# Reordering the first transfers of a Strassen-style GEGLU feed-forward kernel

## The chip, the cores and the metric

The kernel runs on one core of a Trainium2 chip. The metric is the device time of one execution in microseconds (us). The time before is 273.48 us, the median of three runs from 273.24 to 274.23 us. The profiled execution took 273.29 us, and its trace spans 271.5 us from the first to the last instruction. All positions in time below are microseconds from the start of that span.

A core has five engines with instruction streams of their own: TensorE (PE; its weight loads are listed apart as PEld), VectorE (DVE), ScalarE (ACT), GpSimd (POOL) and SyncE (SP). SP and ACT also issue transfers; their issue work is listed as SPq and ACTq. Sixteen DMA engines move the data.

## The reference

All inputs are bf16. The tokens are flattened to 1024 rows.

```python
B, S, D, F = 32, 32, 1024, 3584        # x: (B, S, D); w_gate, w_up: (D, F); w_down: (F, D)

def _gelu(x):
    return jax.nn.gelu(x, approximate=True)

def reference(x, w_gate, w_up, w_down):
    return (_gelu(x @ w_gate) * (x @ w_up)) @ w_down
```

## The kernel before, in words

**What is computed where.** The kernel does both stages (gate and up together, then down) by a Strassen-like scheme of block sums, with products of 128x128 weights against 128x512 moving columns. Stage one treats the gate matrix and the up matrix as two block columns and splits the inner dimension of 1024 into two halves of `KD` = 4 blocks of 128. The transposed activations lie in four tiles, `b11`, `b12` (first half of the inner dimension, token halves 0 and 1) and `b21`, `b22` (second half). Each has 4 blocks of 128 rows and 512 columns.

**The start.** One of the products, the lower half of the gate matrix (`a12`) by `b21`, needs no block sums. The kernel does it ahead for the first 24 blocks of 128 gate columns: six groups of four (`a12_ahead`, indices 0 to 5). Groups 0 and 1 are in tiles named `a12a`, the rest in `a12b`. Each group's tile holds 4 blocks of 128 rows, `k` = 0 to 3, with 512 columns; one such block is 128 KB and is called a gate row block here.

`b21` is filled in two ways. Its blocks 0 and 1 (`KQ` = 2) come as plain copies of x into `x_nat` (`load_nat`, L198, one transfer of 128 KB for each block), are transposed on PE against an identity matrix (`transposed`, L262), and are copied out of PSUM by DVE (L269). Its blocks 2 and 3 come by one transposing transfer (`load_xT(0, KD + KQ, DT)`, L226, issued at L219). The other three tiles of x come by transposing transfers later on.

**What sets the order.** The order is written out by hand: inside `tc.manual_schedule()` each engine runs its instructions in program order, and semaphores between engines and transfers are derived from the tiles that are read and written. Transfers issued by one engine go through that engine's queue in order. Before the change the queues begin so:

- SP: block 0 of `x_nat` (L205); group 0, `k` = 0 (L223); group 0, `k` = 1 (L225); the transposing transfer for blocks 2 and 3 of `b21` (L226); group 0, `k` = 2 and 3; group 1, `k` = 2 and 3 (L230); groups 2 and 3 in halves; the first chunk's up and gate weights (L238); group 4; two more transposing transfers; group 5; the last transposing transfer; the second chunk's weights.
- ACT: a probe of 0.5 KB (L208); block 1 of `x_nat` (L224); group 1, `k` = 0 and 1 (L227); then a table load and a one-column `gelu` (L254) that brings the table in before it is needed.
- POOL: constants and the identity matrix; then nothing until the first block sums, which wait for up weights.

PE begins with `NWARM` = 6 matmuls on constants (L258). It transposes block 0 (four transposes, L266), runs `NFILL` = 4 short matmuls on constants (L273), and goes into the loop at L331:

```python
for k in range(KQ):
    for half in range(2):
        for j in range(KB):
            product_ahead(ps[0][j], 0, j, k, k + 1, slice(half * HALF * P, (half + 1) * HALF * P))
        if k == half == 0:
            transposed(1)
for j in range(KB):
    product_ahead(ps[1][j], 1, j, 0, KQ)
for i in (0, 1):
    for j in range(KB):
        product_ahead(ps[i][j], i, j, KQ)
```

So the needs come in this order: group 0 `k` = 0 with block 0 of `b21`; block 1 of `x_nat`; group 0 `k` = 1; group 1 `k` = 0 and 1; then blocks 2 and 3 of `b21` with group 0 `k` = 2 and 3; then group 1 `k` = 2 and 3; then groups 2 to 5 and the chunks (L368). All matmuls of the products have line L288 or L277 in the profile, since helpers record them.

Of the kernel before, what the change touches and what calls it, by code (L numbers as in the profile page):

```python
# [8 lines left out]
ACT = mybir.ActivationFunctionType  # L9
# [4 lines left out]
def kernel(  # L14
# [20 lines left out]
    nc = tc.nc  # L35
    P = nc.NUM_PARTITIONS
    fp32 = mybir.dt.float32
    f32r = mybir.dt.float32r
    bf16 = mybir.dt.bfloat16
# [7 lines left out]
    NB = 512  # L47
    assert N == 2 * NB and D == 2 * NB and F % (4 * P) == 0
    DT, FT = D // P, F // P
    KD = DT // 2  # L50
# [4 lines left out]
    KQ = DT // 4  # L55
    HF = FT // 2
    MT = NB // P
    NWARM = 6
    NFILL = 4
    KB = 4  # L60
    QF = HF // 2
    batches = [(0, KB), (KB, QF), (QF, QF + KB), (QF + KB, HF)]
# [12 lines left out]
    ework = one.enter_context(tc.tile_pool(name="ework", bufs=2))  # L75
# [37 lines left out]
    a12_ahead = [ring.tile([P, KD, KB * P], bf16, name="a12a", tag="ring") for _ in range(2)]  # L113
    b11 = xpool.tile([P, KD, NB], bf16, name="b11")
    b21 = xpool.tile([P, KD, NB], bf16, name="b21")
# [74 lines left out]
    ident = xpool.tile([P, P], bf16, name="ident")  # L190
    make_identity(nc, ident)
    NB_P = NB // P
# [4 lines left out]
    with tc.manual_schedule():  # L197
        def load_nat(eng, dt, p0, p1):  # L198
            eng.dma_start(  # L199
                out=x_nat[:, p0:p1, dt * P : (dt + 1) * P],  # L200
                in_=xf[p0 * P : p1 * P, (KD + dt) * P : (KD + dt + 1) * P].rearrange("(b p) d -> p b d", p=P),
            )
# [7 lines left out]
        def load_ahead(i, k0, k1, eng=nc.sync, j0=0, j1=KB):  # L210
            f0 = i * KB
            eng.dma_start(
                out=a12_ahead[i][:, k0:k1, j0 * P : j1 * P],
                in_=wg_r[:, KD + k0 : KD + k1, (f0 + j0) * P : (f0 + j1) * P],
            )

        def load_xT(nb, d0, d1):
            t = ((b11, b12), (b21, b22))[d0 // KD][nb]
            nc.sync.dma_start_transpose(  # L219
                out=t[:, d0 % KD : (d1 - 1) % KD + 1, :], in_=xf[nb * NB : (nb + 1) * NB, d0 * P : d1 * P]  # L220
            )

        load_ahead(0, 0, 1)  # L223
        load_nat(nc.scalar, 1, 0, NB_P)  # L224
        load_ahead(0, 1, 2)  # L225
        load_xT(0, KD + KQ, DT)  # L226
        load_ahead(1, 0, KQ, nc.scalar)  # L227
        a12_ahead += [spool.tile([P, KD, KB * P], bf16, name="a12b", tag=t) for t in ("s2", "s4", "s1", "s3")]
        for i in (0, 1):
            load_ahead(i, KQ, KD)  # L230
        def load_halves(i):
            for k in range(0, KD, KQ):
                load_ahead(i, k, k + KQ)
# [3 lines left out]
        for which in (1, 0):  # L237
            load_w_all(0, which)  # L238
        load_ahead(4, 0, KD)
        load_xT(0, 0, KD)  # L240
        load_xT(1, 0, KD)
        for j0 in range(0, KB, KB // 2):
            load_ahead(5, 0, KD, j0=j0, j1=j0 + KB // 2)
# [1 line left out]
        for which in (1, 0):  # L245
            load_w_all(1, which)

        def gelu(src, tag, bufs):
            h = ework.tile([P, NB], bf16, name=tag, tag=tag, bufs=bufs)[:, : src.shape[-1]]
            nc.scalar.activation(h, src, ACT.Gelu_apprx_tanh)  # L250
            return h


        gelu(ident[:, :1], "h0", 6)  # L254

        warm_ps = acc("A")
        for _ in range(NWARM):
# [4 lines left out]
        def transposed(dt):  # L262
            for half, tp in enumerate(tps[dt]):
                p0 = half * HALF
                for b in range(HALF):
                    nc.tensor.transpose(  # L266
                        tp[:, b * P : (b + 1) * P], x_nat[:, p0 + b, dt * P : (dt + 1) * P], ident
                    )
                nc.vector.tensor_copy(b21[:, dt, p0 * P : (p0 + HALF) * P], tp)  # L269

        transposed(0)
        for _ in range(NFILL):
            nc.tensor.matmul(warm_ps[:, :P], lhsT=ones_w, rhs=ones_w, start=True, stop=True)  # L273
# [41 lines left out]
        def first_product(ft):  # L315
            psa = acc("A")
            prod(psa, quads(*chunk_of(ft))[0], b11, True)
            if ft < NAHEAD:
                return psa, gelu(added(ahead_at[ft], psa), "h0", 6)
            return psa, snap(psa, "sn1", 4)  # L320
# [34 lines left out]
        tt(t2, b22, t1, SUB)  # L355
        group_ahead(5, "CCAA", between=lambda: nc.scalar.copy(b22r, b22))
        begun = {ft: (psa, gelu(c, "h0", 6)) for ft, (psa, c) in begun.items()}
        tt(t3, b22, b12, SUB)
        next(chunk0)
# [8 lines left out]
        for ci in range(NCH):  # L368
# [8 lines left out]
            sn5, sn2, h1, h0 = [], [], [], []  # L377
# [17 lines left out]
            if fts[-1] < NAHEAD:  # L395
                h0 = first
# [228 lines left out]
```

## Time and profile before

| What | Value |
|---|---|
| Time, median of three runs | 273.48 us |
| Time of the profiled execution | 273.29 us |
| Its span | 271.5 us |
| PE busy | 267.4 us (98%) |
| DVE busy | 202.8 us (75%) |
| ACT busy | 115.6 us (43%) |
| POOL busy | 120.2 us (44%) |
| Granted TensorE clock, mean | 1.000 |
| Bytes moved by DMA | 35.86 MB, 132 GB/s on average |

Busy shares are of the span. A matmul's recorded duration includes the fill and drain of the array and overlaps the next one, so the pace of a run of matmuls is read from start to start. A transfer has two times: how long the issuing engine is occupied (the SPq and ACTq entries) and how long after the begin of the issue its data has landed (the median in the table of issues). Where a group of issues is only one transfer, the median is that transfer's own time.

### The profile page before, as it was taken

Reading aid. Unit: us, or ns where it says so; the run is one execution under the profiler, and the core shown is the slowest. Engines: PE = TensorE matmul, PEld = TensorE weight load, DVE = VectorE, ACT = ScalarE, POOL = GpSimd, SP = SyncE. Lnnn points to the kernel's source line nnn. Section 1 sums busy time; section 2 is a strip of 40 time slices with the busy share of each in tenths; the row PEclk is TensorE's granted clock in tenths of the full one; section 3 lists DMA queues with packets and bytes.
Section 4 is the critical chain, followed back from the end, with each engine's and each line's share of the span. In section 5 each row is a group of like instructions: output and inputs, shape, how many; then the busy total and the mean of one; then the engine's idle time right before and its main releaser. Section 6 shows DMA issues by size and latency. Waiting matters only on the chain.

```text
span 271.5 us, 3422 instructions
## 1 busy us (share of the span) xinstructions
PE 267.4 (98%) x1216; PEld 192.9 (71%) x1216; DVE 202.8 (75%) x205; ACT 115.6 (43%) x189; POOL 120.2 (44%) x60
## 2 busy tenths in 40 slices
PE   8999999999999999999999999999999999999995
PEld 4444776886787788688688687764458888888883
DVE  1448998886876876876776478469999999998621
ACT  2435766445544643745636635434000307870000
POOL 1090099977995994994994996000000000000000
DMA  7999230514505505505224290006981537865211
GB/s 173 325 245 251 52 104 21 150 38 117 157 1 153 156 2 155 139 15 157 81 76 127 49 325 4 0 2 202 356 253 60 158 112 260 273 196 163 73 42 58
DMA packets 56672, 35.86 MB, mean 132 GB/s; under 512 B 9936, under 2 KB 56656, under 8 KB 56656
## 3 DMA queue, kind: packets, MB, share of 16 engines
q1 hardware_dynamic: 53264, 33.17, 43.2%
q10 hardware_dynamic: 3392, 2.49, 2.8%
q8 instruction: 9, 0.15, 0.2%
q14 instruction: 7, 0.06, 0.1%
HBM read 31.72 MB, written 2.10 MB: 125 GB/s over the span
## 4 chain that ended last, share of the span: by engine, by line
PE 97%; DMA 1%; SPq 0%; DVE 0%; issue 0%
PE psA L277 38%; PE psA L429 24%; PE psC L277 19%; PE psC L429 7%; PE psA L288 5%; PE psC L288 3%; DMA a12a<-in_w_gate_dram 1%; PE psC L593 1%; SPq L199 0%; DVE o_last L594 0%; PE tp L266 0%
## 5 line engine op out<-in xcount | busy, mean ns | idle before, releaser
L277 PE MATMUL psA<-t,s 128*128 128x512 f32 x224 | 57.2, 397 | 0.0
L250 ACT ACTIVATE h<-c 128x512 bf16<-128x512 f32 x56 | 34.6, 629 | 41.6 <-DVE c L307 41.6
L277 PEld LDWEIGHTS psA<-t,s 128*128 128x128 f32 x224 | 42.1, 188 | 9.5
L171 POOL TENSOR_TENSOR s<-wu 128x1024 fp32r<-128x1024 bf16 x13 | 29.5, 2270 | 30.6 <-DMA wu<-in_w_up_dram 19.7
L172 POOL TENSOR_TENSOR s<-s,wg 128x1024 fp32r<-128x1024 f32 x14 | 32.0, 2284 | 15.0 <-DVE s L171 13.9
L277 PE MATMUL psA<-b,wg 128*128 128x512 bf16 x128 | 29.4, 380 | 0.0
L174 POOL TENSOR_TENSOR s<-wg,wu 128x1024 fp32r<-128x1024 bf16 x13 | 28.4, 2182 | 0.0
L277 PE MATMUL psA<-t,a22r 128*128 128x512 f32 x112 | 27.9, 391 | 0.0
L277 PE MATMUL psC<-t,s 128*128 128x512 f32 x112 | 27.9, 391 | 0.0
L277 PE MATMUL psC<-b22r,s 128*128 128x512 f32 x112 | 27.7, 389 | 0.0
L307 DVE TENSOR_TENSOR c<-sn,psA 128x512 f32<-128x512 f32 x32 | 21.8, 683 | 6.7 <-PE psA L277 5.9
L312 ACT COPY sn<-psC 128x512 f32<-128x512 f32 x28 | 16.3, 588 | 21.9 <-PE psC L277 14.9
L277 PEld LDWEIGHTS psC<-t,s 128*128 128x128 f32 x112 | 21.0, 188 | 4.5
L277 PEld LDWEIGHTS psA<-t,a22r 128*128 128x128 f32 x112 | 21.0, 188 | 4.5
L277 PEld LDWEIGHTS psC<-b22r,s 128*128 128x128 f32 x112 | 21.0, 188 | 4.4
L307 DVE TENSOR_TENSOR c<-sn,psC 128x512 f32<-128x512 f32 x28 | 19.2, 688 | 6.4 <-PE psC L277 6.4
L277 PEld LDWEIGHTS <-wg 128*128 128x128 bf16 x128 | 11.8, 98 | 15.3 <-issue 2.4
L406 DVE TENSOR_TENSOR lo<-c,h 128x512 bf16<-128x512 f32 x14 | 21.3, 1522 | 0.9
L173 POOL TENSOR_TENSOR s<-wg,s 128x1024 fp32r<-128x1024 bf16 x10 | 21.6, 2159 | 0.8
L312 ACT COPY sn<-psA 128x512 f32<-128x512 f32 x32 | 18.3, 592 | 5.5 <-PE psA L277 5.4
L307 DVE TENSOR_TENSOR c<-ahead,psA 128x512 f32<-128x512 f32 x24 | 16.4, 688 | 4.0 <-PE psA L277 2.4
L325 DVE TENSOR_TENSOR hi<-h,psA 128x512 bf16<-128x512 bf16 x14 | 9.6, 687 | 11.5 <-PE psA L277 11.5
(87 smaller groups left out, 381.1 us busy)
## 6 DMA issues: line engine op xcount, KB each, us to landing
wu<-in_w_up_dram SPq DMA_DIRECT2D x14, 512.0 KB, 4.0
wdb<-in_w_down_dram SPq DMA_DIRECT2D x12, 512.0 KB, 4.4
wg<-in_w_gate_dram SPq DMA_DIRECT2D x9, 512.0 KB, 5.1
wdb<-in_w_down_dram SPq DMA_DIRECT2D x12, 384.0 KB, 4.4
v<-in_w_down_dram SPq DMA_DIRECT2D x4, 512.0 KB, 6.2
out_dram<-o_sb ACTq DMA_DIRECT2D x15, 128.0 KB, 1.7
a12b<-in_w_gate_dram SPq DMA_DIRECT2D x6, 256.0 KB, 4.8
wg<-in_w_gate_dram SPq DMA_DIRECT2D x6, 256.0 KB, 4.7
```

Of the source, the lines that this page charges most:

```text
L171: yield engs[0].tensor_tensor(s1, a21, a22, ADD)
L172: yield engs[1].tensor_tensor(s2, s1, a11, SUB)
L173: yield engs[2].tensor_tensor(s4, a12, s2, SUB)
L174: yield engs[3].tensor_tensor(s3, a11, a21, SUB)
L250: nc.scalar.activation(h, src, ACT.Gelu_apprx_tanh)
L277: nc.tensor.matmul(ps, lhsT=lhs[:, k, :], rhs=rhs[:, k, :], start=(start and k == 0), stop=(k == KD - 1), skip_group_check=True,)
L288: nc.tensor.matmul(ps[:, cols], lhsT=a12_ahead[i][:, k, j * P : (j + 1) * P], rhs=b21[:, k, cols], start=(k == 0 and not cols.start), stop ...
L307: tt(t, s, ps, ADD)
L312: nc.scalar.copy(t, ps)
L325: tt(g_of(ft)[:, :NB], h0, psa, MUL)
L406: tt(g_of(ft)[:, NB:], added(sn5[fl], psa[fl]), h1[fl], MUL)
L429: nc.tensor.matmul(banks[m], lhsT=lhs(k)[:, m * P : (m + 1) * P], rhs=rhs(k), start=(start and k == 0), stop=(k == HF - 1), skip_group_che ...
```

## The change

Four things are edited.

1. ACT: the one-column `gelu` (with its table load) moves from behind ACT's transfers to ahead of the transfer of group 1, `k` = 0 and 1. ACT no longer issues block 1 of `x_nat`.
2. SP: block 1 of `x_nat` is issued by SP, between group 0's `k` = 0 and `k` = 1. Group 0's `k` = 2 is issued right behind `k` = 1, as a transfer of 128 KB of its own.
3. POOL gets a copy of one element, from the first gate row block (group 0, `k` = 0) to the first element of block 2 of `b21`. The transposing transfer overwrites that element, so SP issues it only after the copy, and the copy runs only after the gate row block has landed. Behind the transposing transfer, SP issues group 0 `k` = 3 (128 KB), then group 1 `k` = 2 and 3 (256 KB), and the rest as before.
4. `NFILL` is 3 instead of 4.

```diff
-    NFILL = 4
+    NFILL = 3
...
+        def gelu(src, tag, bufs):
+            h = ework.tile([P, NB], bf16, name=tag, tag=tag, bufs=bufs)[:, : src.shape[-1]]
+            nc.scalar.activation(h, src, ACT.Gelu_apprx_tanh)
+            return h
+
+        gelu(ident[:, :1], "h0", 6)
+
         def load_xT(nb, d0, d1):
...
+        load_ahead(1, 0, KQ, nc.scalar)
         load_ahead(0, 0, 1)
-        load_nat(nc.scalar, 1, 0, NB_P)
+        load_nat(nc.sync, 1, 0, NB_P)
         load_ahead(0, 1, 2)
+        load_ahead(0, KQ, KQ + 1)
+        nc.gpsimd.tensor_copy(b21[:1, KQ, :1], a12_ahead[0][:1, 0, :1])
         load_xT(0, KD + KQ, DT)
-        load_ahead(1, 0, KQ, nc.scalar)
         a12_ahead += [spool.tile([P, KD, KB * P], bf16, name="a12b", tag=t) for t in ("s2", "s4", "s1", "s3")]
-        for i in (0, 1):
-            load_ahead(i, KQ, KD)
+        load_ahead(0, KQ + 1, KD)
+        load_ahead(1, KQ, KD)
...
-        def gelu(src, tag, bufs):
-            h = ework.tile([P, NB], bf16, name=tag, tag=tag, bufs=bufs)[:, : src.shape[-1]]
-            nc.scalar.activation(h, src, ACT.Gelu_apprx_tanh)
-            return h
-
-
-        gelu(ident[:, :1], "h0", 6)
```

## The prediction

> **What bounds the kernel now.** I read the page's busy times first, then the waits of PE, then the chain that ended last over its first microseconds, and then the timeline and the table of issues for the start, since the edits lie there.
>
> ```profile
> PE 267.4 (98%) x1216; PEld 192.9 (71%) x1216; DVE 202.8 (75%) x205; ACT 115.6 (43%) x189; POOL 120.2 (44%) x60
> ```
>
> ```profile
> PE psA L258 <- PEq L609: 0.8, 1, 0.8
> PE psC L288 <- DMA a12a<-in_w_gate_dram: 0.5, 1, 0.5
> ```
>
> ```profile
> 1.24 3.41 DMA a12a<-in_w_gate_dram
> 4.65 0.05 issue
> 4.70 0.39 PE psC L288 x2
> ```
>
> PE is the bound: it is idle for 271.5 - 267.4 = 4.1 us. Of these 0.8 lie ahead of its first instruction, 0.5 are a wait for the first gate row block, and the rest (from 268.63, when the last matmul ends, to 271.5) is the final addition and store. So the only idle time that this change can reach is the half microsecond before 4.70, and the constant matmuls just ahead of it. From 4.70 on PE has no gap, so each later transfer of the start already meets its need, and what matters is by how much.
>
> ```profile
> 1.22 0.53 ACTq L199 DMA_DIRECT2D x_nat<-in_x_dram  x1
> 1.24 0.96 SPq L212 DMA_DIRECT2D a12a<-in_w_gate_dram  x2
> 1.78 0.53 ACTq L212 DMA_DIRECT2D a12a<-in_w_gate_dram  x1
> 2.25 1.34 SPq L219 DMA_TRANSPOSE b<-in_x_dram  x1
> 2.34 1.28 ACT L250 ACT_TABLE_LOAD   x1 [2.34 <-issue]
> ...
> 3.71 0.49 PE L273 MATMUL psA<-const-bfloat16-1.0 128*128 128x128 bf16 x4
> 3.74 0.51 DVE L269 COPY b<-tp 128x256 bf16<-128x256 bf16 x2 [3.74 <-PE tp L266]
> ...
> 5.17 0.40 PE L266 MATMUL tp<-ident,x_nat 128*128 128x128 bf16 x4
> ```
>
> ```profile
> x_nat<-in_x_dram SPq DMA_DIRECT2D x1, 128.0 KB, 2.4
> ```
>
> ```profile
> x_nat<-in_x_dram ACTq DMA_DIRECT2D x1, 128.0 KB, 3.9
> a12a<-in_w_gate_dram SPq DMA_DIRECT2D x1, 128.0 KB, 3.4
> ```
>
> ```profile
> a12a<-in_w_gate_dram ACTq DMA_DIRECT2D x1, 256.0 KB, 4.5
> a12a<-in_w_gate_dram SPq DMA_DIRECT2D x1, 128.0 KB, 3.7
> b<-in_x_dram SPq DMA_TRANSPOSE x1, 4.9
> ```
>
> Issue time plus time to landing gives the arrivals, and PE's rows give the needs. Block 0 of x_nat lands at 0.73 + 2.4 = 3.1. The first gate row block lands at 4.65 and is used at 4.70. Block 1 of x_nat lands at 1.22 + 3.9 = 5.12 and is used at 5.17. Gate row `k` = 1 lands at 1.78 + 3.7 = 5.5, used at 5.84. Group 1 lands at 1.78 + 4.5 = 6.3, used at 6.71. The transposing transfer lands at 2.25 + 4.9 = 7.15, used at 8.44. These use times are also the points of break-even: PE is full behind them, so a transfer that lands later than its use time before makes the kernel slower, whatever was won earlier.
>
> **The change, part by part.**
>
> First gate rows. By windows of half a microsecond, between 2.5 and 3.5 the DMA engines move 158 to 199 GB/s at a share of 0.74 to 1.03, and at 4.0 to 5.0 some 345 to 350 GB/s. The first stretch carries x_nat (pieces of 256 bytes), the second gate rows. So x_nat costs about 128 KB at 180 GB/s = 0.7 us of all engines, a gate row block 128 KB at 350 = 0.4 us. Now ACT's x_nat block is in flight beside the first gate rows, and they land half a microsecond apart, at 5.12 and 4.65. With the block behind those rows on one queue, the rows have only x_nat block 0 ahead. Their landing is bounded below by that transfer's own 2.4 us (1.24 + 2.4 = 3.64) and above by no change (4.65). I take 3.65, as the engines then have 0.4 us of work for it behind a transfer landing at 3.1.
>
> Cited beside this: the Trainium skill, DMA: Bandwidth & Descriptors (Queues, rings and completion order), says that each DMA engine takes turns between the queues that have work, packet by packet. That agrees with 4.65 and 5.12. The same page (Issuing engines are not separate DMA queues) says that the issuing engine matters only for issue time; read strictly, the move gains nothing, and 4.65 would stay.
>
> What PE can use of it. The constant matmuls and four transposes end in the same place. DVE's first copy runs 3.74 to 4.03 (0.29 each), and 0.06 on, at 4.09, the first product can start. Three short matmuls at their start-to-start pace of 0.107 (3.71, 3.82, 3.92) end by 4.03, so the fourth, which would have ended at 4.20, must go for this, and its removal costs nothing. Gain: 4.70 - 4.09 = **0.61 us**. Even rows that land at 3.64 give no more: the copy is late next. All later needs move up by 0.61, to 4.56 for x_nat block 1, 5.23 for `k` = 1, 6.10 for group 1, 7.83 for the transposing transfer.
>
> x_nat block 1 is issued by SP at about 1.78 instead of 1.22. Bounds: 1.78 + 2.4 = 4.2 and 1.78 + 3.9 = 5.7, a stall between 0 and 1.1 us. I take 4.25: 0.7 us of engine work behind the gate rows, in front of everything else. `k` = 1 follows at 2.25 (bounds 4.65 to 5.95; I take 4.7), and `k` = 2, issued at about 2.75, has until 7.83.
>
> ACT. Its queue passes from the probe (ends 1.19) to the table load (1.28) and the activation (0.21), so group 1's transfer is issued at about 2.8 instead of 1.78. The identity that the activation reads is ready at 1.30, well inside the load. Bounds: 2.8 plus 3.5, the fastest 256 KB row (a half of group 5), or plus 4.5, so 6.3 to 7.3 against a need of 6.10: a stall of 0.2 to 1.2. But both rows wait behind other work. Counted as a stream, from 3.9 on `k` = 1, `k` = 2 and this are 512 KB, 1.5 us at 350 GB/s, so 5.4, and 5.7 to 5.8 with the 0.3 from last data to landing that x_nat block 0 shows. I take 5.8, without stall. Taking the load away from 2.34 to 3.64 saves nothing: ACT is next wanted at 9.07.
>
> The Trainium skill, ScalarE: Activation LUTs (What ACT_TABLE_LOAD costs), adds a drain of about 1.38 us to the load of 1.28; here the activation starts 0.02 after the load, so the trace shows none. With it group 1 would land near 7.2.
>
> The transposing transfer and its queue. SP waits from about 3.2 for the gate rows (3.65), then for POOL's copy of one element (0.1 to 0.2 us, by POOL's small rows, and about 0.1 of hand-overs), so it issues at 3.9 instead of 2.25. POOL is otherwise idle until 13.74, so its wait is free. Issue takes 1.34. From issue's end to landing the four transposing transfers show 3.56, 3.5, 2.2 and 2.0 (the last, 512 KB, issued 19.68 for 3.28 and landing 5.3 after its begin). So it lands between 3.9 + 1.34 + 2.0 = 7.24 and 8.8; the largest row, 8.8 us from begin to landing, would make it 12.7. I take 2.2, landing at 7.45, 0.4 ahead of its need: in all, 1152 KB have then passed, against about 1216 KB by 7.0 in the trace before (summed from its windows), so no backlog is larger.
>
> Behind it on SP everything is issued about 1.6 us later. First is `k` = 3, needed one matmul (0.22) after the transposing transfer, at 8.05. Before, 256 KB landed 0.8 behind it, so 128 KB land 0.4 behind, at 7.85. Next is group 1's second half, 0.75 later at 8.6, as before; its need moves from 10.17 to 9.56. Groups 2 and 3 were landing 2 us or more ahead. Of the later tiles of x, the last lands at 25.0 and feeds a DVE sum that ends at 27.42 for a matmul at 29.28, which leaves 1.9. A full 1.6 plus 0.61 would eat that, but SP ran 4 to 7 us ahead of landings there, so I cost it at nothing.
>
> Sum against the profiled execution: 273.29 - 0.61 = 272.7. The median of the runs is 0.19 above the profiled one, so 273.48 - 0.6 = **272.9**.
>
> **Rivals.** Half a per cent, 1.4 us, is about what a measurement of this kernel can tell from no change, so most cases fall within it.
>
> The gain is eaten by arrivals just behind (273.2 to 273.7). The slacks that I worked out are 0.2 to 0.4 us, and x_nat block 1, group 1 or `k` = 3 late by 0.3 to 0.7 gives most of the 0.6 back. For it: x_nat block 1 had 0.05 to spare before. Against it: less is in flight ahead of each. That the gate rows land at 4.65 regardless ends here too.
>
> The transposing transfer is late (273.8 to 274.8, and beyond). It is the one transfer that waits now, and decides from 8.44: with a tail of 3.56 it lands at 8.8, a stall of 0.97 and a net loss of 0.36; if the gate rows come at 4.2 to 4.65, 9.3 to 9.8, a loss of 0.9 to 1.35. Slower by over 1.4 needs a landing after 9.8, for which only the row of 8.8 us speaks; that would be 277.7. Against it: long tails were seen with a full queue ahead.
>
> The clock. The start-to-start pace of PE's short matmuls goes from 0.107 to 0.06 at about 3.95 (they start at 3.71, 3.82, 3.92 and 3.98), just before the new start. If it opens 0.5 later, work in 4.09 to 4.45 runs at half pace and 0.2 of the gain is gone. The Trainium skill, TensorE: Matmul & The Clock Gate (What you observe), gives such a spread; no run here shows it.
>
> **How the numbers follow.** The forecast, 0.3 to 0.7 us faster, has 0.57. The gain eaten has 0.23; the late clock 0.04 of this. The late transposing transfer has 0.16: 0.06 within 1.4 us, and 0.10 beyond, since no row shows its tail behind a wait. Faster by over 1.4 us has 0.04, as PE has no idle time that could give it. So faster 0.04, same 0.86, slower 0.10. The range runs from 272.4 (0.6 gained and half a microsecond from what the runs vary) to 274.4, which leaves out 0.04 below and about 0.14 above, among them some of the smaller losses.
>
> **What would show it.** First product row near 4.1 with no wait on the gate rows; the transposing transfer issued near 3.9 and landed before 7.8; group 1's transfer issued near 2.8 behind the table load; PE without gaps to 8.5. A wait of PE at L288 on `b`, or at L266 on x_nat, after 4.1 would show the first two rivals. I am wrong if the first rows still land after 4.5, or the transposing transfer lands after 8.44.

## The result and the profile after

The kernel after takes 274.76 us (median of nine runs, 274.41 to 276.88), the kernel before 273.68 us in the runs beside it. The ratio is 1.0050, with an interval from 1.0031 to 1.0068: slower by 1.1 to 1.4 us, where 0.6 us faster was forecast. The profiled execution took 275.09 us and spans 273.3 us, 1.8 us more than that of before. The two profiled executions lie 0.4 us below their kernel's median (before) and 0.3 us above it (after), so about 0.7 of these 1.8 us is what executions of one kernel vary by. The sums below account for the two traces, not for the medians.

The page's busy times and PE's waits in the kernel after (waits: who waited for whom, total, times, longest, in us):

```profile
PE 267.9 (98%) x1202; PEld 192.7 (71%) x1215; DVE 202.6 (74%) x205; ACT 115.6 (42%) x189; POOL 120.8 (44%) x61
```

```profile
PE psA L260 <- PEq L611: 0.8, 1, 0.8
PE psC L290 <- DMA a12b<-in_w_gate_dram: 0.5, 1, 0.5
PE tp L268 <- DMA x_nat<-in_x_dram: 0.3, 1, 0.3
```

The wait for the first gate rows is gone from PE's list. Two others stand in its place: the second transposes wait for block 1 of x_nat, and far later, group 5 of a12 (`a12b`) is late. The timeline of the start (begin, duration, engine, line, operation) and the landing of three transfers:

```profile
1.21 1.28 ACT L219 ACT_TABLE_LOAD   x1 [1.21 <-PEq L611]
1.25 0.50 SPq L212 DMA_DIRECT2D a12a<-in_w_gate_dram  x1
1.34 0.41 ACTq L212 DMA_DIRECT2D a12a<-in_w_gate_dram  x1
1.79 0.43 SPq L199 DMA_DIRECT2D x_nat<-in_x_dram  x1
...
4.31 0.61 PE L290 MATMUL psC<-b,a12a 128*128 128x256 bf16 x2
4.32 0.18 POOL L235 COPY b<-a12a 1x1 bf16<-1x1 bf16 x1 [3.01 <-DMA a12a<-in_w_gate_dram]
4.52 1.33 SPq L226 DMA_TRANSPOSE b<-in_x_dram  x1
4.71 0.64 PE L290 MATMUL psA<-b,a12a 128*128 128x256 bf16 x2
...
5.68 0.40 PE L268 MATMUL tp<-ident,x_nat 128*128 128x128 bf16 x4 [0.33 <-DMA x_nat<-in_x_dram]
```

```profile
a12a<-in_w_gate_dram ACTq DMA_DIRECT2D x1, 256.0 KB, 3.9
a12a<-in_w_gate_dram SPq DMA_DIRECT2D x1, 128.0 KB, 3.0
x_nat<-in_x_dram SPq DMA_DIRECT2D x1, 128.0 KB, 3.8
```

```profile
b<-in_x_dram SPq DMA_TRANSPOSE x1, 3.2
```

The first gate rows land at 4.27 (issued at 1.25, and 3.02 to landing by the chain below) instead of 4.65, and the first product starts 0.39 earlier. ACT issues group 1's transfer at 1.34, in the middle of its table load, so it is ahead of block 1 of x_nat, which lands at 1.79 + 3.8 = 5.6. The transposing transfer lands at 4.52 + 3.2 = 7.7, before its use.

The chain that ended last, in the kernel after, over its first 40 us (begin, duration, what). Before, this chain ran over PE from 4.70 to the end. Now it runs over SP's issues up to 21.1:

```profile
1.25 3.02 DMA a12a<-in_w_gate_dram
...
4.52 1.33 SPq L226
5.85 0.05 issue
5.90 0.57 SPq L212
...
12.86 5.06 SPq L226
17.92 0.04 issue
17.97 3.08 SPq L226
21.05 0.04 issue
21.09 4.02 DMA a12b<-in_w_gate_dram
25.12 0.05 issue
25.16 1.90 PE psC L290 x8
```

```profile
34.52 1.14 issue
35.66 0.60 DVE s L171
36.26 0.53 issue
36.79 1.41 DVE c L309 x3
```

Read the gaps between SP's pieces: 0.04 to 0.05 us, all the way. SP's rows show no idle time between the transposing transfer and group 5. The profile of before shows the same if one adds its rows up (2.25 + 1.34 = 3.59, next at 3.63; 4.71, next at 4.76; and so on to 18.51). In this stretch SP's waits name no other transfer that it waited for, so the longer pieces (5.06 us for one issue) are not waits for a semaphore, the counter by which a transfer reports its landing. What stretches them the profile doesn't say. That SP's rows have no gap doesn't show that SP could not have caught up: the run with SP's issues moved to ACT, below, made up time.

The lateness at the start is still there at group 5 and at the tiles of x. Before:

```profile
18.51 1.13 SPq L212 DMA_DIRECT2D a12b<-in_w_gate_dram  x2
20.80 2.29 DVE L349 TENSOR_TENSOR t<-b,b 128x2048 fp32r<-128x2048 bf16 x1 [1.10 <-DMA b<-in_x_dram]
23.98 1.89 PE L288 MATMUL psC<-b,a12b 128*128 128x512 bf16 x8
```

and after:

```profile
21.09 1.13 SPq L212 DMA_DIRECT2D a12b<-in_w_gate_dram  x2
23.20 2.29 DVE L351 TENSOR_TENSOR t<-b,b 128x2048 fp32r<-128x2048 bf16 x1 [3.00 <-DMA b<-in_x_dram]
25.16 1.90 PE L290 MATMUL psC<-b,a12b 128*128 128x512 bf16 x8 [0.51 <-DMA a12b<-in_w_gate_dram]
```

The same PE rows in both traces give the sum. The first products start 0.39 earlier, but the four of them take 0.83 us (4.31 to the end of the fourth, begun at 4.93) instead of 0.47, at the slow pace: -0.03. PE then waits until 5.68, which was 5.17: +0.51, and this stands unchanged until 22.77 (22.25 before). Group 5's first product starts at 25.16 instead of 23.98: +1.18. From 27 to 43 DVE's sums of the x tiles, begun at 23.20 instead of 20.80, hold PE up once more: +1.75 at 45.51 (43.76 before), and it is +1.75 at the last products too (267.15 and 265.40).

### The profile page after: what moved, and what is told of

It reads as the page before. It is cut to its first block, busy times and chain, and to the rows that moved or that the text cites. A ratio compares the mean times of both kernels' runs of the same rounds, so it can differ in the third digit from the quotient of the medians.

```text
span 273.3 us, 3411 instructions
## 1 busy us (share of the span) xinstructions
PE 267.9 (98%) x1202; PEld 192.7 (71%) x1215; DVE 202.6 (74%) x205; ACT 115.6 (42%) x189; POOL 120.8 (44%) x61
## 4 chain that ended last, share of the span: by engine, by line
PE 87%; SPq 6%; DMA 3%; issue 2%; DVE 2%; POOL 0%; DVEq 0%
PE psA L279 35%; PE psA L431 24%; PE psC L279 18%; PE psC L431 7%; SPq L226 3%; SPq L212 2%; DMA a12b<-in_w_gate_dram 1%; DVE c L309 1%; PE psC L595 1%; DMA a12a<-in_w_gate_dram 1%; PE psC L290 1%; PE psA L290 1%; SPq L136 1%; DVE s L171 0%; SPq L199 0%
## 5 line engine op out<-in xcount | busy, mean ns | idle before, releaser
L174 POOL TENSOR_TENSOR s<-wg,wu 128x1024 fp32r<-128x1024 bf16 x13 | 29.4, 2261 | 0.0
L279 PE MATMUL psA<-b,wg 128*128 128x512 bf16 x119 | 27.8, 379 | 0.6
L279 PE MATMUL psC<-b22r,s 128*128 128x512 f32 x112 | 27.8, 390 | 0.0
L408 DVE TENSOR_TENSOR lo<-c,h 128x512 bf16<-128x512 f32 x14 | 21.1, 1505 | 0.9
L408 DVE TENSOR_TENSOR hi<-c,h 128x512 bf16<-128x512 f32 x14 | 17.8, 1271 | 0.9
```

What stands on the lines that cost most here:

```text
L174: yield engs[3].tensor_tensor(s3, a11, a21, SUB)
L279: nc.tensor.matmul(ps, lhsT=lhs[:, k, :], rhs=rhs[:, k, :], start=(start and k == 0), stop=(k == KD - 1), skip_group_check=True,)
L408: tt(g_of(ft)[:, NB:], added(sn5[fl], psa[fl]), h1[fl], MUL)
```

## The experiments

The first question was which of two things makes the loss. Theory W: the wait of the transposing transfer delays all that SP issues behind it, and group 5 and the x tiles pay for it. Theory Q: the order of the first transfers makes block 1 of x_nat late, and all that follows is only shifted. Within W, the second question was what is short while SP waits: SP's own issue time (theory S) or the DMA engines, which are left with too little to do (rival D).

Each kernel's ratio is to the kernel before, run beside it on the same chip. The marks, in us, are from the profiled execution of each. "SP transposing" is the issue of the first transposing transfer, "second transposes" PE's work on block 1 of x_nat, "k = 2" the first product on the transposed blocks, "group 5" SP's first issue for it, "last" the last products' start. Slow or fast is the start-to-start pace of the first four products (about 0.21 or 0.11 us). One profile shows one execution: "both undone" and "undone, relieved" issue the same transfers and run the same instructions on PE up to their first products, and yet their first gate rows land at 4.3 and 3.8 and their pace turns fast near 3.5 and 5.9. A difference of that size between two profiles can't be put down to an edit.

| Kernel | SP transposing | first product | second transposes | k = 2 | group 5 | last | ratio (95% interval) |
|---|---|---|---|---|---|---|---|
| before | 2.25 | 4.70 fast | 5.17 | 8.44 | 18.51 | 265.40 | 1 |
| after | 4.52 | 4.31 slow | 5.68 | 8.95 | 21.09 | 267.15 | 1.0050 (1.0031 to 1.0068) |
| no wait | 3.26 | 4.53 slow | 5.61 | 8.95 | 19.24 | 265.97 | 1.0017 (1.0005 to 1.0029) |
| wait alone | 4.36 | 4.15 slow | 4.99 | 9.49 | 20.42 | 266.49 | 1.0043 (1.0027 to 1.0059) |
| group 1 behind | 4.11 | 4.07 fast | 4.50 | 8.27 | 20.47 | 266.18 | 1.0023 (1.0001 to 1.0046) |
| table first | 2.24 | 4.14 slow | 13.48 | 19.47 | 19.36 | 276.48 | 1.0344 (1.0314 to 1.0373) |
| both undone | 3.77 | 4.37 fast | 4.90 | 8.17 | 20.46 | 266.37 | 1.0019 (1.0006 to 1.0031) |
| SP relieved | 3.82 | 4.02 fast | 4.92 | 10.62 | 19.23 | 268.35 | 1.0132 (1.0092 to 1.0171) |
| four fillers | 4.47 | 4.26 slow | 5.49 | 9.12 | 20.36 | 266.68 | 1.0053 (1.0035 to 1.0071) |
| undone, relieved | 3.78 | 4.09 slow | 4.90 | 8.63 | 19.52 | 269.95 | 1.0165 (1.0137 to 1.0193) |
| one x transfer | 2.26 | 4.60 fast | 5.04 | 8.30 | 18.55 | 265.32 | 0.9998 (0.9979 to 1.0016) |
| transposing third | 2.72 | 4.14 slow | 4.99 | 8.43 | 18.49 | 265.42 | 1.0006 (0.9990 to 1.0022) |
| both of these | 2.71 | 4.72 fast | 5.19 | 8.69 | 18.72 | 265.64 | 1.0018 (0.9994 to 1.0042) |
| four small issues | 4.46 | 4.18 slow | 5.04 | 9.56 | 21.04 | 266.56 | 1.0062 (1.0039 to 1.0085) |

### Without the wait

```diff
 (against after)
-        nc.gpsimd.tensor_copy(b21[:1, KQ, :1], a12_ahead[0][:1, 0, :1])
```

> The kernel after without the one-element copy on POOL, so that the transposing transfer is issued as soon as SP reaches it (about 3.3 instead of 4.52); all else as after. Theory W (the wait delays all that SP issues behind it, and this is paid at group 5 of a12 and in DVE's sums of x): the first half of group 5 lands before 24.0 again, PE has no wait there, and the time falls by 1.0 to 1.3 us from after, to 273.4 to 273.8. Theory Q (the loss is made at the start, by the order of the first transfers: group 1 of a12 goes out ahead of block 1 of x_nat, and what follows only shifts): PE's second transposes stay near 5.7 and the time stays at 274.5 to 274.9. If both are true: transposes near 5.7, no wait at group 5, and 274.0 to 274.3.

Measured: 273.95 us, ratio 1.0017, so about 0.9 us of the 1.4 us loss are gone. Group 5 is issued at 19.24 and PE doesn't wait for it. The second transposes stay at 5.61. PE is 0.44 us behind before there, 0.51 behind at `k` = 2 and 0.57 behind at the last products. These are the marks of the case that both theories are true, with a time 0.05 below that case's range: theory W gives the larger part, theory Q the rest.

### The wait alone

```diff
 (against before)
+        nc.gpsimd.tensor_copy(b21[:1, KQ, :1], a12_ahead[0][:1, 0, :1])
         load_xT(0, KD + KQ, DT)
```

> The kernel before with only the one-element copy on POOL ahead of the transposing transfer. Theory W: the transposing transfer is issued near 5.0 instead of 2.25, group 5 lands later than 24.5, and the time is 1.0 to 1.8 us above before, 274.7 to 275.5. Theory Q: the start up to the second transposes is as before or slightly earlier, and the time is within 0.3 us of before, 273.4 to 274.0.

Measured: 274.68 us, ratio 1.0043. The one line costs nearly as much as the whole change, as theory W forecast. Theory W's mark for group 5 is not met: it landed at 20.42 + 3.4 = 23.8. The kernel pays at another place than the kernel after: group 0's `k` = 2 and 3, issued behind the transposing transfer at 5.75 instead of 3.63, are late (first product on them 9.49 instead of 8.44). After that PE is itself so late that group 5 is in time. The kernel after had moved `k` = 2 in front of the wait, which avoids this, and meets the bill at group 5 instead. Part of this profile's delay is the slow pace, which lasts to about 6.5 here.

The first gate rows are used at 4.15 here, although block 1 of x_nat is still issued by ACT at 1.21. So block 1 beside them, to which the prediction had put it down, need not keep them until 4.65. The transposing transfer behind them is not shown to be the cause either: in the kernel with the table load alone it is issued at 2.24, as before, and the rows are used at 4.14, with ACT's two transfers out of the way. On the Trainium skill, DMA: Bandwidth & Descriptors (Issuing engines are not separate DMA queues), the prediction said that, read strictly, moving the block gains nothing. The first products at 4.15 without the move and 4.31 with it don't contradict that.

### Group 1 behind block 1 of x_nat

```diff
 (against after)
-        load_ahead(1, 0, KQ, nc.scalar)
...
         load_ahead(0, 1, 2)
+        load_ahead(1, 0, KQ)
         load_ahead(0, KQ, KQ + 1)
```

> The kernel after with group 1 of a12 (k = 0 and 1) issued by SP behind group 0 k = 1, not by ACT beside the table load; the wait of the transposing transfer stays. Both theories: block 1 of x_nat lands near 4.3 instead of 5.6, and PE's second transposes start near 4.7 instead of 5.68. Theory Q: what is won there stays to the end, and the time falls by 0.7 to 1.0 us, to 273.7 to 274.1. Theory W: group 5 still lands near 25.1, PE waits for it up to 1.5 us instead of 0.5, and the time stays at 274.5 to 275.0.

Measured: 274.11 us, ratio 1.0023. The landing of block 1, from the issues of this kernel:

```profile
x_nat<-in_x_dram SPq DMA_DIRECT2D x2, 128.0 KB, 2.5
```

Two transfers, 2.4 and 2.6 us: block 1 lands at 1.78 + 2.6 = 4.4, against 5.6 with group 1's 256 KB ahead of it, and the second transposes start at 4.50. So group 1's early issue by ACT made block 1 late. The start is now as the prediction drew it: first product at 4.07, transposes at 4.50. Yet PE is 0.09 behind before at group 5 (24.07) and 0.78 behind at the last products, as DVE's sums start at 22.57 instead of 20.80. What was won at the start is gone, and SP's lateness takes the rest. The time fell by about 0.7 us from after, close to what theory Q forecast, and theory W's condition did not come about: PE has no wait for group 5, though SP issues it at 20.47. So the two theories don't divide the loss cleanly.

### The table load alone

```diff
 (against before)
+        gelu(ident[:, :1], "h0", 6)
         def load_xT(nb, d0, d1):
...
-        gelu(ident[:, :1], "h0", 6)
```

> The kernel before with only the one-column gelu and its table load moved to the front of ACT's stream, ahead of block 1 of x_nat and group 1 of a12. If ACT issues transfers while the table loads, as the kernel after shows it (issue at 1.34 inside the load from 1.21 to 2.49), block 1 of x_nat is issued near 1.3 and the time is that of before within 0.3 us (273.4 to 274.0). If a load holds the queue after all, as the prediction took it, block 1 of x_nat is issued near 2.8, the second transposes start near 6.5, and the time is 1.2 to 1.5 us above before.

Measured: 282.81 us, ratio 1.0344, which neither expectation held. From the chain that ended last in this kernel:

```profile
2.24 3.73 DMA b<-in_x_dram
5.97 0.02 issue
5.99 7.45 DMA x_nat<-in_x_dram
13.44 0.05 issue
13.48 0.61 PE tp L265 x4
```

ACT issues block 1 of x_nat at 5.99, when the transposing transfer has landed, though it has no data in common with it. The semaphores recorded in the trace explain it: transfers of both engines share eight of them in turn, and each transfer waits for the one that held its semaphore before. With an activation ahead of it, block 1 came later in that order, and its semaphore had been the transposing transfer's. Block 1 then takes 7.45 us beside SP's transfers. The table load itself ends at 2.49, as in the kernel after, where group 1's transfer has no such wait and goes out inside the load. So the table load did not hold ACT's transfer there; a move among the transfers can, through the shared semaphores. Part of this kernel's loss is pace: PE waits 8.3 us for block 1, the granted clock is 0.50 from 10 to 19 us, and the matmuls of that stretch run slow.

### Both losses undone

```diff
 (against after)
-        load_ahead(1, 0, KQ, nc.scalar)
-        nc.gpsimd.tensor_copy(b21[:1, KQ, :1], a12_ahead[0][:1, 0, :1])
...
+        load_ahead(1, 0, KQ)
```

> The kernel after without the one-element copy, and with group 1 of a12 issued by SP behind group 0 k = 1. If the two losses (the wait: 0.9 us between after and the kernel without it; group 1 ahead of block 1 of x_nat: 0.75 us) are separate and add, the time falls by 1.5 to 1.7 us from after, to 273.0 to 273.3, a little below before. If they overlap, one of them filling what the other leaves (SP issues without a pause from its first transfer to near 24, so whatever starts earlier only waits for it later), the time is 273.5 to 274.0, no better than before.

Measured: 274.42 us, ratio 1.0019. They overlap: no better than either alone, and above the ranges of both cases. With group 1 on SP, SP has three issues more ahead of the transposing transfer than before (block 1, group 1, and `k` = 2), and issues it at 3.77 without any wait. Group 5 goes out at 20.46, as late as with the wait. PE waits 0.6 us for group 1's second half and then loses more in DVE's sums. (This profile's execution, at 276.18 us, was the slowest of thirteen.)

### SP's issues moved to ACT

```diff
 (against the kernels with group 1 behind)
-        load_ahead(1, KQ, KD)
-        load_halves(2)
+        load_ahead(1, KQ, KD, nc.scalar)
+        load_halves(2, nc.scalar)
```

With the wait of the transposing transfer kept:

> As the run with group 1 behind block 1 of x_nat (the wait of the transposing transfer stays), but the second half of group 1 and both halves of group 2 are issued by ACT, three issues of about 0.5 us off SP's stream. Theory S (SP's own issue time is the resource that the wait costs; SP is never idle until 24): SP's first issue for group 5 moves from 20.5 to about 19.0, the loss in DVE's sums between 27 and 43 goes, and the time falls by 0.5 to 0.8 us from that run, to 273.3 to 273.6. Rival D (the DMA engines, left dry while SP waited, are the resource): what SP issues later lands when the engines get to it, group 5 and the x tiles land as in that run within 0.3 us, and the time stays at 274.0 to 274.3.

Without it:

> Group 1 behind block 1 of x_nat, no wait for the transposing transfer, and three issues moved from SP to ACT: what is left of the change is the early start. If SP's issue time and the arrival of block 1 of x_nat explain the loss, nothing is late any more behind a first product near 4.1, and the time is 0.3 to 0.7 us below before, 272.9 to 273.3. If the early start is worth nothing (another wait takes it up), it is that of before, 273.5 to 273.8.

Measured: 277.55 us (1.0132) and 278.15 us (1.0165). Both fail as tests, since the three transfers brought new waits with them. In the first kernel PE's waits are

```profile
PE psC L290 <- DMA b<-in_x_dram: 2.3, 1, 2.3
PE psA L260 <- PEq L611: 0.8, 1, 0.8
PE psC L290 <- DMA a12a<-in_w_gate_dram: 0.6, 1, 0.6
PE tp L268 <- DMA x_nat<-in_x_dram: 0.3, 1, 0.3
```

The transposing transfer, issued at 3.82, is used only at 10.62, with ACT's transfers of 256 KB (3.59 and from 5.31 on) in flight beside it. In the second, ACT's own issues come only at 6.00 and 8.00, by the shared semaphores, and PE waits 1.3 us for group 1 and 2.5 us for group 2. The first kernel still says something about SP. Among SP's waits it has

```profile
SPq L136 <- DMA b<-in_x_dram: 3.2, 1, 3.2
```

and yet group 5 was issued 1.2 us earlier than in the kernel with group 1 behind (19.23 against 20.47). SP so made up 3.2 + 1.2 = 4.4 us. Of these, the three issues taken away are about 1.5 and the earlier start of the transposing transfer is 0.3; for the rest the issues behind the wait were shorter. So SP could make up time. It gained nothing by it: the first half of group 5 landed at 19.23 + 4.7 = 23.9 against 20.47 + 3.5 = 24.0, and the last tile of x at 21.31 + 5.6 = 26.9 against 21.64 + 5.2 = 26.8. That is what rival D forecast for the landings. With the new waits in the way it is a hint and no test.

### Four short matmuls

```diff
 (against after)
-    NFILL = 3
+    NFILL = 4
```

> The kernel after with four short constant matmuls instead of three. If the missing one lets the clock of PE open later (in the profile of after the first four products run at the slow pace, in that of before at the fast one), the first four products run fast again and the time falls by up to 0.3 us. If the opening comes at its own time (it was seen near 3.6, 3.95, 5.2 and 6.3 in kernels with the same first matmuls), the time is that of after within 0.2 us, 274.6 to 274.9, since PE waits for block 1 of x_nat near 5.6 either way.

Measured: 275.20 us, ratio 1.0053: as after by the ratio, 0.3 us above the expected range. The products are slow until about 6.3 with four as well, so the slow pace does not need the missing matmul.

### Four small issues

```diff
 (against before)
+        for t in small:                       # four tiles of 0.5 KB, never read
+            nc.sync.dma_start(out=t, in_=wg_r[::4, KD:, :2])
         load_xT(0, KD + KQ, DT)
```

> The kernel before, with four transfers of 0.5 KB each (as the probe) issued by SP ahead of the transposing transfer: they move next to no data, cost SP about 0.45 us each, and the program makes every transfer wait for the one eight earlier, so the transposing transfer goes out near 4.5 to 5 instead of 2.25, as late as in the kernel after, with block 1 of x_nat and group 1 of a12 as before. If SP's lateness alone costs (theory S), group 5 of a12 is issued 2.0 to 2.6 us later and the time is 0.7 to 1.4 us above before, 274.4 to 275.1. If only the DMA engines' load matters, nothing that they carry has changed, and the time is within 0.3 us of before.

Measured: 274.86 us, ratio 1.0062. No data to speak of is added, no wait on the gate rows, block 1 and group 1 are issued as before, and the loss of the whole change is there. The timeline of SP and PE in this kernel:

```profile
2.26 1.86 SPq L228 DMA_DIRECT2D small<-in_w_gate_dram  x4
...
4.46 1.33 SPq L220 DMA_TRANSPOSE b<-in_x_dram  x1
...
9.56 1.04 PE L291 MATMUL psC<-b,a12a 128*128 128x512 bf16 x4 [0.80 <-DMA a12a<-in_w_gate_dram]
```

Four issues cost 1.86 us of SP, 0.47 each, and 0.3 more is a wait of the transposing transfer, for block 1 of x_nat, which held its semaphore before. Nothing is caught up: SP is 2.2 us late here and 2.5 us late at group 5 (21.04). The kernel as a whole loses 1.3 us by the medians and 1.7 by the ratio. Like the kernel with the wait alone, it pays first at group 0's `k` = 2 and 3. So a late SP is enough for the loss, whatever makes it late. This run doesn't decide between theory S and rival D, although it was meant to. While SP issues transfers that carry nothing, the DMA engines run dry as well: their busy share is 0.16 from 5 to 6 us and 0.56 from 7 to 8 (0.44 and 0.67 in the kernel after, 1.23 and 1.11 before). (The share adds up packets that overlap, so it can pass 1.) In the kernel after it stays lower up to 13 us (0.88 to 1.03 from 8 on, 1.10 to 1.20 before), and from 13 to 16 the two are alike, 1.10 to 1.22: so up to 16 us the engines make up little of what they missed. In the trace of before, the halves of groups 2 and 3 are issued 0.51 us apart and land 0.75 apart (issued at 4.76, 5.27, 5.78 and 6.29, and 4.7, 4.9, 5.3 and 5.5 to landing): there the engines, not SP, set the pace of the landings. That spacing favours rival D, but no run here separates the two.

### Two edits for a faster start

One transfer for both blocks of x_nat, on SP:

```diff
 (against before)
-                out=x_nat[:, p0:p1, dt * P : (dt + 1) * P],
+                out=x_nat[:, p0:p1, dt * P : (dt + KQ) * P],
...
-        load_nat(nc.scalar, 1, 0, NB_P)
```

> The kernel before, with both blocks of x_nat in one transfer of 256 KB on SP (pieces of 512 bytes instead of 256), and ACT's transfer of block 1 gone; all else as before. If the start is set by the arrival of the gate rows and of block 1 behind each other's small pieces, the one transfer lands by 3.4, the first product starts at 4.1 to 4.4, the second transposes follow without a wait, SP issues nothing more than before, and the time falls by 0.3 to 0.6 us, to 273.0 to 273.4. If the larger first transfer delays the first transposes past 3.28 by more than it saves, the first product is at 4.7 or later and the time is 273.6 to 274.2.

Measured: 273.34 us, ratio 0.9998: no difference. The 256 KB land 2.9 us after their issue (128 KB took 2.4), so the first transposes start at 3.72 instead of 3.28 and the products at 4.60, 0.1 earlier than before; PE's lead is 0.1 from there on.

Group 0's `k` = 2 and 3 ahead of the transposing transfer:

```diff
 (against before)
-        load_xT(0, KD + KQ, DT)
         load_ahead(1, 0, KQ, nc.scalar)
+        load_ahead(0, KQ, KD)
+        load_xT(0, KD + KQ, DT)
```

> The kernel before, with group 0 k = 2 and 3 issued ahead of the transposing transfer instead of behind it; no wait, and as many issues. If the transposing transfer behind them is what makes the first gate rows late (they land at 4.65 with it issued at 2.25, at 4.1 to 4.3 in the kernels that issue it after 3.2), they land near 4.3, and SP's stream behind is in time: 0.1 to 0.4 us below before, 273.2 to 273.6. If what is gained there is taken by the transposing transfer landing after 8.1, or the rows land at 4.65 all the same, the time is that of before or up to 0.4 us above.

Measured: 273.46 us, ratio 1.0006: no difference. Its profile has the first product at 4.14, 0.56 earlier, with SP's stream in time (group 5 at 18.49), and yet `k` = 2 starts at 8.43, as before. The first four products run at the slow pace (4.14, 4.35, 4.57, 4.78), and the second transposes are still slow; the lead is gone at 5.39. The early start was spent at half pace in this execution. Whether others with an earlier opening keep it, one profile can't say; the lowest of its twelve runs, 272.80, is that of before, 272.82.

Both together:

> Both of the last two edits together. If they help in different places they add: 0.5 to 0.8 us below before, 272.8 to 273.2, with the first product at 4.1. If PE then waits for group 1 or the transposing transfer, 273.2 to 273.7.

Measured: 273.62 us, ratio 1.0018, an interval that includes 1. The first product is at 4.72. No kernel of the study is measurably faster than the one before.

## Why the prediction was wrong

**The bound, and the idle time within reach: right.** PE's half microsecond ahead of 4.70 was all there was, and no run was faster than before beyond its interval.

**"All later needs move up by 0.61": wrong by size.** The first rows landed at 4.27, not 3.65 (within the bounds given), with 0.39 gained at the first product. The four products then took 0.36 longer at the slow pace. This is the rival of the clock, given 0.04: in eight of the fourteen profiles of the table the first products run at the slow pace. The openings, where the pace turns fast, lie from about 3.5 (group 1 behind, both undone) to about 6.5 (wait alone). The Trainium skill, TensorE: Matmul & The Clock Gate (What you observe), gives a spread of half a microsecond to each side, for matmuls without a pause; here PE pauses between its first matmuls, and the traces are wider than that.

**"Its queue passes from the probe to the table load and the activation, so group 1's transfer is issued at about 2.8": wrong.** It went out at 1.34, as soon as the identity was ready (1.30), while the table was loading. That put 256 KB ahead of block 1 of x_nat, which landed at 5.6, at the far end of the bounds 4.2 to 5.7, not at the 4.25 taken. The value was worked out with nothing from ACT in flight. The kernel with group 1 behind shows the size: block 1 lands at 4.4 there. Cost: 0.51 us at PE.

**"SP ran 4 to 7 us ahead of landings there, so I cost it at nothing": the step that decided.** The distance from issue to landing was read as slack. It was none: what was issued later also landed later. The first tile of x landed at 12.86 + 8.6 = 21.5 instead of 10.29 + 8.8 = 19.1, the last at 22.27 + 5.5 = 27.8 instead of 19.68 + 5.3 = 25.0. The later issue was foreseen as 1.6 us; it was 2.27 us at the transposing transfer (two issues more, and 1.3 us of wait) and 2.58 us at group 5, which the prediction's list of needs left out altogether. The x tiles' slack of 1.9 was named, with the remark that a full delay would eat it. It did: +0.67 at group 5, +0.57 in DVE's sums. Four issues that carry nothing reproduce the loss. Why the lateness was not caught up stays open: SP's own issue time, or work that the DMA engines missed from 5 us on and did not make up, as the landings suggest.

**The transposing transfer: right.** It landed 3.2 us after a 4.52 issue, with a tail of 1.9 behind the issue's end (2.2 was taken), and PE did not wait for it. The rival that the wait makes the kernel slower had the right culprit and the wrong victim: not the waiting transfer was late, but those behind it. With other traffic beside it (SP relieved: issued at 3.82, used at 10.62) the transfer was late.

**The range:** its upper end of 274.4 lies 0.4 us below the median. The rival of the late transposing transfer, with 0.16, reached to 274.8 and was cut off; a delay of what stands behind the wait had no case of its own.

## What to carry to other kernels

Before a wait or a transfer is added to a queue, don't take the time from issue to landing as slack: here a delay of 2.3 us at one issue was a delay of 2.4 to 2.8 us at the landings of the x tiles. Look at the queue's rows and at the DMA engines' busy share together: rows without a gap alone don't say which of the two is short. List the needs of everything behind the insertion, to the end of the full stretch, and not only of the next few transfers. An engine's transfers may go out earlier than its program order suggests and later than their data needs: look for what releases each.

## What the runs showed of the hardware that was not expected

- ACT issued a transfer at 1.34, inside a table load from 1.21 to 2.49.
- A transposing transfer of 256 KB of blocks 2 and 3 occupied SP for 1.33 to 1.49 us in all the kernels, against 0.4 to 0.6 us for a plain transfer of 0.5 to 512 KB when nothing held it (four small issues: 0.47 each).
- Transfers of SP and ACT shared eight semaphores, so that a transfer of one engine could wait for an unrelated one of the other (table first: block 1 of x_nat issued at 5.99 instead of 1.22).
- The landing of the first gate rows varied by 0.5 us (4.3 and 3.8), and the opening of PE's fast pace by 2.4 us (3.5 and 5.9), between profiles of two kernels that are the same up to there (both undone; undone, relieved).
- After the transposing transfer the DMA engines of the kernel after moved a third as much, 119 and 121 GB/s in two half microseconds in which they moved 352 before. In the windows of the two traces (stretch, length, busy time of PE, PEld, DVE, ACT, POOL, clock, DMA share, GB/s), before:

```profile
7.00:7.50 0.50, 0.50 (x4) 0.22 (x3) 0.00 (x0) 0.00 (x0) 0.00 (x0) 1.00 1.11 352
7.50:8.00 0.50, 0.50 (x4) 0.20 (x2) 0.00 (x0) 0.00 (x0) 0.00 (x0) 1.00 1.11 352
```

and after:

```profile
7.00:7.50 0.50, 0.50 (x6) 0.35 (x4) 0.00 (x0) 0.00 (x0) 0.00 (x0) 1.00 0.78 119
7.50:8.00 0.50, 0.50 (x4) 0.23 (x3) 0.00 (x0) 0.00 (x0) 0.00 (x0) 1.00 0.57 121
```

The column of the granted clock reads 1.00 in the starts where PE's pace was half. That is no measurement: the clock's records in the trace of after begin only at 5.66, and the trace of before has none.
